# A quarter-by-quarter second product put ahead of the next batch, with the loads in another order

## The chip, the cores and the metric

The kernel runs on one core of one Trainium2 chip. The metric is the device time of one execution in microseconds, and the median of several runs is given. A profile is one more execution, with every instruction and every DMA packet recorded.

The engines are TensorE (PE in the profile; PEld is its weight loads), VectorE (DVE), ScalarE (ACT), GpSimd (POOL) and SyncE (SP). They run side by side and wait for each other by semaphores. In this kernel SP issues the loads of q, k and v and the DMA transpositions, and POOL issues the loads of the weights and most of the output stores.

## The reference

Eight batches go through a linear attention and then a mixer. Cut to what is computed:

```python
# attention: batch, heads, seq, head_dim = 8, 8, 576, 64
r = max(x, 0);  phi(x) = concat(r * cos_w, r * sin_w)       # for q and for k, cos_w and sin_w by position
kv  = einsum('bhsf,bhsd->bhfd', phi(k), v)
num = einsum('bhsf,bhfd->bhsd', phi(q), kv)
den = einsum('bhsf,bhf->bhs', phi(q), sum(phi(k), axis=2)) + 1e-6
x   = num / den                                             # heads side by side: (8, 576, 512)
# mixer: U (576, 32), V (32, 576), w_ch1 (512, 2048), w_ch2 (2048, 512)
u   = x + (x^T @ U @ V)^T
out = u + max(u @ w_ch1, 0) @ w_ch2
```

Inputs and output are float32; the kernel multiplies in bfloat16 and sums in float32.

## The kernel before

**Tiles.** The 576 rows of a batch are four chunks of 128 (c = 0 to 3, row 4p + c on partition p) and a tail of 64 (c = 4). Tails of two batches share the partitions of one tile, so batches go in pairs (`pr`, batches `e` = 2 pr and `o` = 2 pr + 1).

**Attention of a batch** is made of units:
- `q_prep` and `k_prep` (two instructions each, one with the cosine and one with the sine, on the engines that the call names), `v_prep` or `v_block` (casts of v into `v_ext`, which has a column of ones, so that kv also holds the sum over phi(k)).
- `qtr_unit`: eight transpositions of a chunk of q on PE and one evacuation. `kv_unit`: 20 small products for four heads.
- x, in one of two ways. `x_unit` makes all eight heads of a chunk with 65 columns each, so the denominators come with the numerators; `den_unit` and `xh_unit` make the denominators of all chunks first, with 20 one-column products, and then x for four heads at a time.
- `A_unit` (x^T U, four column groups of PE side by side), `u_unit` (A V and the sum with x), and u transposed for the next product, either by PE (`uTd_open`, `uTd_mm`, `uTd_evac`: x transposed, A V added in the same accumulator) or by a DMA (`utr_dma`). `uTt_direct` does the pair's tail on PE.

**The mixer.** `g1_main(b, j)` is one of 16 units of the first product of a batch: four matmuls of 128x512, then the evacuation with the relu by ACT into `hid`. It needs the j-th 128 columns of `w1_bf`, which is loaded in quarters (`w1_load(n)`, columns for four units each). `g1_tail` does four units for both tails. `g2_part(pr, cc, p)` is a quarter of the second product for one chunk: four matmuls with four of the 16 row blocks of `w2_bf`, which is loaded in quarters too (`w2_load(n)`). After the fourth part DVE adds u and a DMA stores the result. Both weights are cast to bfloat16 by the DMA, so that a quarter is 0.52 MB in the core and 1.05 MB outside.

**Order.** The schedule is written out by hand: instructions of an engine run in the order in which the code calls them. First comes batch 0's attention (`chain_head`, `chain_mid`, `chain_end`), with `keep_warm` products on zeros between. Then a list of slots runs: for each pair 16 units of `g1_main` for the even batch, 16 for the odd, four of `g1_tail`, and 36 of `g2_part` (nine chunks by four parts), 72 slots in all. After each slot the calls stand that are attached to it: those of `beside` (batch 1) and those that `attention_plan` derives from `PLAN` (batches 2 to 7: the slot of the first kv unit, then the offsets of the casts, the transpositions and the next batch's loads). In the first pair slots 8 to 12 are empty, since batch 1's chain, called at slot 7, holds these five units inside itself (`fill1`).

**Memory for sums.** Eight PSUM banks: tag "o" has two buffers, "g" three, "T" one, and "X" one of two banks. A unit names the tag that it takes, and waits until the buffer's last reader is done.

**Loads.** q, k and v of a batch have one buffer each (`qst`, `kst`, `vst`, with the tails in `qt`, `kt`, `vt`), so the next batch's load waits until the casts have read the last. SP issues them in the order of the code. POOL issues the weights: the first quarter of `w1` once k of batch 0 has landed (a copy into `mark`, line 685, waits for it), the second after batch 0's chain head, which on POOL means after the casts of U and V (`cast_uv`); the third and fourth after a copy that waits for the transposed tail of batch 1's q (line 722); the quarters of `w2` after one that waits for batch 1's v (line 724). A one-element DMA into `mark2` (line 647) holds batch 2's loads back on SP until batch 1's second denominators are made.

Of the kernel before, what the change touches and what calls it, by code (L numbers as in the profile page):

```python
# [10 lines left out]
FP32 = mybir.dt.float32  # L11
# [6 lines left out]
def kernel(  # L18
# [11 lines left out]
    nc = tc.nc  # L30
# [31 lines left out]
    def alloc_k(b):  # L62
        kst[b] = pool.tile([P, H, 4, D], FP32, tag="kst", bufs=1, name="kst")
        kt[b] = pool.tile([P, H, D], FP32, tag="kt", bufs=1, name="kt")
# [9 lines left out]
    def load_main(dst, src, b, h0=0, h1=H, eng=None):  # L74
        (eng or nc.sync).dma_start(
            out=dst[:, h0:h1, :, :].rearrange("p h c d -> p h (c d)"),
            in_=src[b, h0:h1, 0:512, :].rearrange("h (p c) d -> p h (c d)", c=4),
        )

    def load_tail(dst, src, b, eng=None):  # L80
        (eng or nc.sync).dma_start(  # L81
            out=dst[tail(b), :, :],
            in_=src[b, :, 512:S, :].rearrange("h s d -> s h d"),
        )
# [4 lines left out]
    def w1_load(n):  # L89
        cs = slice(n * 512, n * 512 + 512)  # L90
        nc.gpsimd.dma_start(
            out=w1_bf[:, :, cs], in_=moe_w_ch1.rearrange("(d p) n -> p d n", p=P)[:, :, cs]
        )
# [36 lines left out]
    load_tail(vt[0], v, 0)  # L130
    load_main(vst[0], v, 0, 0, 4)
    load_main(vst[0], v, 0, 4, 8)
    for i in range(4):
        nc.sync.dma_start(out=stV[i * R : i * R + R, :], in_=moe_V)
    nc.sync.dma_start(
        out=stU[:, 0:4, :], in_=moe_U[0:512, :].rearrange("(p c) r -> p c r", c=4)
    )
    for lo in (0, TS):
        nc.sync.dma_start(out=stU[lo : lo + TS, 4, :], in_=moe_U[512:S, :])
    zero = const.tile([P, 512], BF16)  # L140
    V_.memset(zero, 0.0)
    halfpi = const.tile([P, 1], FP32)
# [33 lines left out]

    V_.memset(U_bf, 0.0)
    mark = const.tile([TS, 1], FP32)
    mark2 = const.tile([1, 1], FP32)

    def cast_uv():
        cast(G_, U_bf[:, 0:4, :], stU[:, 0:4, :])
        for i in range(2):
            cast(G_, U_bf[tail(i), 4 + i, :], stU[tail(i), 4, :])
        cast(G_, V_bf, stV[:, 0:512].rearrange("r (p c) -> r c p", c=4))
        cast(G_, V_tl, stV[:, 512:S])
# [242 lines left out]
    def uTd_close(b, d, eng):  # L429
        uTd_mm(b, d)  # L430
        uTd_evac(b, d, eng)
# [75 lines left out]
    def g2_part(pr, cc, part):  # L507

        last = pr == NPAIR - 1 and cc == 8
        if part == 0 or last and part == 3:  # L510
            o_ps[pr, cc] = ps.tile([P, DM], FP32, tag="o", bufs=2, name="o_ps")
        o = o_ps[pr, cc]
        if cc == 4:
            b, lhs, c, u = None, hid_tl[pr], 0, u_tl[pr]
        else:
            b, c = (2 * pr, cc) if cc < 4 else (2 * pr + 1, cc - 5)
            lhs, u = hid[b], u_bf[b][:, c, :]

        if last:
            cols = slice(0, 384) if part < 3 else slice(384, DM)  # L520
            js = (range(0, 5), range(5, 10), range(10, NJ), range(NJ))[part]
        else:
            cols, js = slice(0, DM), range(part * 4, part * 4 + 4)
        for j in js:
            nc.tensor.matmul(  # L525
                out=o[:, cols],
                lhsT=lhs[:, j, c * P : c * P + P],
                rhs=w2_bf[:, j, cols],
                start=(j == 0),
                stop=(j == NJ - 1),  # L530
            )
        if js[-1] < NJ - 1:
            return
        o_sb = pool.tile([P, DM], FP32, tag="o_sb", bufs=4, name="o_sb")
        nc.vector.tensor_tensor(  # L535
            out=o_sb[:, cols], in0=u[:, cols], in1=o[:, cols], op=ALU.add
        )
        eng = nc.gpsimd if pr < NPAIR - 1 else nc.scalar if part == 3 and last else nc.sync
        if cc == 4:
            for i in range(2):  # L540
                eng.dma_start(
                    out=out[2 * pr + i, 512:S, :], in_=o_sb[i * TS : i * TS + TS, :]
                )
        else:
            eng.dma_start(  # L545
                out=out[b, 0:512, cols].rearrange("(p c) n -> p c n", c=4)[:, c, :],
                in_=o_sb[:, cols],
            )
# [20 lines left out]
    ORD = (4, 0, 1, 2, 3)  # L569

    def spare(at):

        return ("o", 2) if at % 72 < 36 else ("g", 3)


# [1 line left out]

    QORD = (4, 0, 1, 2, 3)
    PLAN = {
        2: (42, -22, V_, V_, -14, (-8, -8, -8)),  # L580
        3: (58, -17, A_, A_, -10, (6, 6, 6)),
        4: (100, -20, V_, V_, -12, (-6, -6, -6)),
        5: (130, -20, A_, A_, -13, (-7, -7, -7)),
        6: (172, -20, V_, V_, -12, (-6, -6, -6)),
# [39 lines left out]
    def chain_head(b, fill, xt, engs):  # L624
        v_prep(b, 0, 4, (4,), (engs[0],))
        v_block(b, 0, 4, 0, 3, V_)
        v_block(b, 0, 4, 3, 4, engs[0])
        kv_unit(b, 0, "T", 1)
        fill(0)
        rec0 = den_unit(b, 0, 4, "X", 1)  # L630
        v_prep(b, 4, 8, (4,), (A_,))
        v_block(b, 4, 8, 0, 4, A_)
        fill(1)
        for n, c in enumerate(ORD):
            xh_unit(b, c, 0, 4, rec0, *xt[n])
            if n == 1:
                fill(2)
            if n == 3:
                kv_unit(b, 1, "T", 1, A_)

    def chain_mid(b, fill, xt, dt):
        fill(3)
        m = 3 if b == 0 else 2
        rec1 = den_unit(b, 4, 8, *dt)
        if b == 1:

            nc.sync.dma_start(out=mark2, in_=rec1[0:1, 0, 0:1])
        for n, c in enumerate(ORD[:m]):
            xh_unit(b, c, 4, 8, rec1, *xt[n])
        u01 = ps.tile([P, 2, 512], FP32, tag="X", bufs=1, name="u01")  # L650
        uTd_open(b, 0, None, None, u01[:, 0, :].rearrange("p (c t) -> p c t", c=4))
        uTd_open(b, 1, None, None, u01[:, 1, :].rearrange("p (c t) -> p c t", c=4))
        a0 = A_unit(b, "T", 1, A_, 0, 256)
        fill(4)
        uTd_mm(b, 0)
        uTd_mm(b, 1)
        uTd_evac(b, 0, A_)
        uTd_evac(b, 1, A_)
        for n, c in enumerate(ORD[m:]):
            xh_unit(b, c, 4, 8, rec1, *xt[m + n])  # L660
        fill(5)
        return a0
# [21 lines left out]

    G_.tensor_copy(out=mark, in_=kt[0][0:TS, 0, 0:1])
    w1_load(0)
    cast_uv()
    chain_head(0, warm0, (O2, O2, G3, G3, O2), (A_,))
    w1_load(1)
    alloc_q(1)  # L690
    load_main(qst[1], q, 1)
    load_tail(qt[1], q, 1)
    alloc_k(1)
    load_main(kst[1], k, 1)
    load_tail(kt[1], k, 1)
    alloc_v(1)
    load_tail(vt[1], v, 1)
    load_main(vst[1], v, 1, 0, 4)
    load_main(vst[1], v, 1, 4, 8)
    a0 = chain_mid(0, warm0, (O2, G3, O2, G3, O2), G3)  # L700
    chain_end(0, a0)
    g1_main(0, 0, True)
# [10 lines left out]
    def at(j, *thunks):  # L713
        beside.setdefault(j, []).extend(thunks)

    for n, c in enumerate(ORD):
        if n > 1:
            at(n - 2, lambda c=c, n=n: q_prep(1, c, (V_, A_ if n % 2 == 0 else V_)))
        tg = ("T", 1) if n % 2 else O2
        at(1 + n, lambda c=c, tg=tg: qtr_unit(1, c, eng=V_, tag=tg[0], bufs=tg[1]))  # L720
        at((4, 5, 5, 6, 6)[n], lambda c=c, n=n: k_prep(1, c, (V_, A_)))
    at(2, lambda: G_.tensor_copy(out=mark, in_=q_tlT[0:TS, 0, TS : TS + 1]))
    at(2, lambda: [w1_load(2), w1_load(3)])
    at(6, lambda: G_.tensor_copy(out=mark, in_=vst[1][0:TS, 0, 0, 0:1]))
    at(6, lambda: [w2_load(n) for n in range(4)])
    st1 = {}

    def fill1(n):
        if n in (0, 4):
            u_unit(0, 0 if n == 0 else 1, "o", 2)  # L730
        if n > 0:
            g1_main(0, 7 + n)

    xt1 = (O2, O2, O2, O2, O2)
    at(7, lambda: chain_head(1, fill1, xt1, (V_,)))
    at(7, lambda: st1.update(a=chain_mid(1, fill1, xt1, ("T", 1))))
    at(7, lambda: chain_end(1, st1["a"]))
    at(13, lambda: uTd_close(1, 2, V_), lambda: uTd_close(1, 3, A_))

    slots, todo = [], {}  # L740
    for pr in range(NPAIR):
        e, o = 2 * pr, 2 * pr + 1
        slots += [
            (lambda: None) if pr == 0 and 8 <= j < 13 else lambda j=j, e=e: g1_main(e, j)
            for j in range(NJ)
        ]
        slots += [lambda j=j, o=o: g1_main(o, j) for j in range(NJ)]
        slots += [lambda j=j, pr=pr: g1_tail(pr, j) for j in range(4)]
        slots += [
            lambda cc=cc, p=p, pr=pr: g2_part(pr, cc, p) for cc in range(9) for p in range(4)  # L750
        ]
    for j, ts_ in beside.items():
        todo[j] = list(ts_)
# [1 line left out]
    def put(at, thunk):  # L755
        todo.setdefault(at, []).append(thunk)

    put(17, lambda: uTt_direct(0, "o", 2, V_))
    for n, (b, c) in enumerate([(0, 2), (0, 3)] + [(1, c) for c in ORD]):
        put(18 + n, lambda b=b, c=c: u_unit(b, c, *spare(18)))  # L760
    for n, t in enumerate(loads(2, nc.sync)):
        put((9, 12, 13)[n], t)
    for b in range(2, B):
        for at, t in attention_plan(b):
            put(at, t)
# [34 lines left out]
```

## Time and profile before

| | |
|---|---|
| median of 3 runs | 319.39 us (317.74 to 320.44) |
| the profiled execution: time, span | 320.26 us, 318.5 us |
| PE busy | 306.9 us, 96% of the span |
| DVE, ACT, POOL busy | 148.2, 145.8, 45.7 us |
| largest groups on PE | first product 119.7 us, second product 119.2 us (line 525) |
| moved by DMA | 53.30 MB, 167 GB/s in the mean |

The span reaches from the first to the last instruction of the program. The profiled execution is a little above the median of the timed ones, so a sum made from its rows is set against its own time. PE's busy share is that of the whole span; what the stages lose is seen only in windows. Times in a timeline are from the span's start. The first unit of `g1_main` starts at 23.6 us, the odd batch's first at about 53 us, the pair's tails at 69.2, the second product at 73.0, and the second pair at 110.4.

### The profile page before, as it was taken

The page shows a single profiled execution, that of the slowest core. Times are in us where ns is not written, and L with a number is a line of the kernel's source. Part 1 is how long each engine was busy: PE and PEld are TensorE (multiplying, and loading weights), DVE is VectorE, ACT ScalarE, POOL GpSimd, SP SyncE. Part 2 cuts the span into 40 slices and gives each one's busy share as a digit, 9 for nine tenths or more (in the row PEclk, how much of TensorE's full clock was granted, in tenths as well). Part 3 has the DMA queues.
Part 4 walks back from the last instruction along what each step waited for, and adds up shares of the span by engine and source line. Part 5 has one row for each costly group of instructions (what it writes and reads, how often), then busy time and mean ns, then how long its engine had stood idle before and what let it go on. Part 6 is the DMA issues. An engine that isn't in the chain of part 4 may idle for free.

```text
span 318.5 us, 5777 instructions
## 1 busy us (share of the span) xinstructions
PE 306.9 (96%) x2372; PEld 160.0 (50%) x2372; DVE 148.2 (47%) x325; ACT 145.8 (46%) x241; POOL 45.7 (14%) x85
## 2 busy tenths in 40 slices
PE   8697799999999999999999999999999999999996
PEld 3464464465545444476445444475445444464443
DVE  6667753880567659125615667025525640001211
ACT  4735836567800056658900056659700256650000
POOL 1132400400420113001421220002321100000000
PEclk9999989999999999999999999999999999999999
DMA  7999999579674899952399539911491130001122
GB/s 233 264 303 282 191 188 320 154 174 323 201 178 118 277 306 181 286 176 19 114 240 348 207 97 201 344 69 51 127 205 66 68 82 0 2 0 68 66 91 74
DMA packets 88603, 53.30 MB, mean 167 GB/s; under 512 B 56642, under 2 KB 85698, under 8 KB 88578
## 3 DMA queue, kind: packets, MB, share of 16 engines
q1 hardware_dynamic: 82002, 41.61, 48.6%
q0 software_dynamic: 6432, 11.27, 14.8%
q8 instruction: 18, 0.29, 0.4%
q10 hardware_dynamic: 144, 0.07, 0.1%
q14 instruction: 7, 0.06, 0.1%
HBM read 37.08 MB, written 9.44 MB: 146 GB/s over the span
## 4 chain that ended last, share of the span: by engine, by line
PE 87%; DMA 7%; DVE 2%; SPq 2%; POOL 0%; issue 0%; DVEq 0%; POOLq 0%
PE o_ps L525 39%; PE g_ps L473 34%; PE gt_ps L493 4%; DMA w_bf<-in_moe_w_ch_dram 3%; DMA vst<-in_v_dram 3%; PE kv_ps L246 3%; PE x_ps L340 2%; PE va_ps L385 2%; DMA st_uv<-in_moe_U_dram 2%; SPq L81 1%; PE a_ps L365 1%; DVE k_p L214 1%; DVE v_ext L105 0%; PE va_ps L388 0%; DVE q_pT L105 0%; PE xh_ps L322 0%
## 5 line engine op out<-in xcount | busy, mean ns | idle before, releaser
L482 ACT ACTIVATE hid<-g_ps 128x512 bf16<-128x512 f32 x128 | 76.3, 597 | 117.8 <-PE g_ps L473 117.7
L473 PE MATMUL g_ps<-uT,w_bf 128*128 128x512 bf16 x512 | 119.7, 383 | 1.9 <-DMA w_bf<-in_moe_w_ch_dram 1.9
L525 PE MATMUL o_ps<-w_bf,hid 128*128 128x512 bf16 (+2 forms) x528 | 119.2, 372 | 0.0
L473 PEld LDWEIGHTS <-w_bf 128*128 128x128 bf16 x512 | 48.9, 98 | 59.4 <-issue 2.8
L525 PEld LDWEIGHTS <-hid 128*128 128x128 bf16 x528 | 48.5, 98 | 51.4 <-issue 0.8
L535 DVE TENSOR_TENSOR o_sb<-u_bf,o_ps 128x512 f32<-128x512 bf16 (+2 forms) x33 | 22.1, 669 | 60.1 <-PE o_ps L525 60.0
L545 POOL DMA_DIRECT2D out_dram<-o_sb x24 | 13.2, 549 | 141.2 <-DVE o_sb L535 65.0
L392 DVE TENSOR_TENSOR u_bf<-x_bf,va_ps 128x512 bf16<-128x512 bf16 x32 | 21.9, 685 | 10.1 <-PE va_ps L385 10.0
L105 DVE CAST kv<-kv_ps 128x260 bf16<-128x260 f32 x14 | 6.0, 429 | 35.8 <-PE kv_ps L246 35.8
L350 DVE TENSOR_TENSOR x_bf<-x_ps,rec 128x512 bf16<-128x512 f32 x24 | 16.6, 691 | 0.8
L105 POOL CAST v_ext<-vst 128x512 bf16<-128x512 f32 x24 | 15.1, 663 | 6.0 <-DMA vst<-in_v_dram 4.2
L493 PE MATMUL gt_ps<-uT_tl,w_bf 128*128 128x128 bf16 x256 | 15.6, 219 | 0.0
L297 DVE TENSOR_SCALAR rec<-x_ps 128x8 f32<-128x8 f32 (+1 forms) x30 | 5.0, 166 | 22.7 <-PE x_ps L340 22.3
L246 PE MATMUL kv_ps<-v_ext,k_p 128*128 128x65 bf16 x256 | 11.9, 193 | 3.4 <-DVE v_ext L105 3.4
L493 PEld LDWEIGHTS <-w_bf 128*128 128x128 bf16 x256 | 14.7, 98 | 0.9
L246 PEld LDWEIGHTS <-k_p 128*128 128x128 bf16 x256 | 11.2, 97 | 7.1 <-ACT v_ext L103 2.1
L525 PE MATMUL o_ps<-w_bf,hid_tl 128*128 128x512 bf16 x64 | 14.8, 379 | 0.0
L175 PE MATMUL w_ps<-zero 128*128 128x512 bf16 x40 | 11.9, 432 | 1.8 <-DVE halfpi L143 1.2
L212 ACT ACTIVATE k_p<-kst,sinw 128x512 bf16<-128x512 f32 x19 | 13.1, 710 | 1.1 <-DMA kst<-in_k_dram 1.1
L212 ACT ACTIVATE q_p<-qst,sinw 128x512 bf16<-128x512 f32 x17 | 11.9, 711 | 3.7 <-DMA qst<-in_q_dram 3.7
L385 PE MATMUL va_ps<-A_sb,V_bf 128*128 128x512 bf16 x32 | 12.1, 379 | 0.1
L500 ACT ACTIVATE hid_tl<-gt_ps 128x512 bf16<-128x512 f32 x16 | 9.6, 598 | 5.8 <-PE gt_ps L493 5.8
(103 smaller groups left out, 243.0 us busy)
## 6 DMA issues: line engine op xcount, KB each, us to landing
qst<-in_q_dram SPq DMA_DIRECT2D x8, 1024.0 KB, 6.8
kst<-in_k_dram SPq DMA_DIRECT2D x8, 1024.0 KB, 9.1
vst<-in_v_dram SPq DMA_DIRECT2D x6, 1024.0 KB, 9.0
out_dram<-o_sb POOLq DMA_DIRECT2D x24, 256.0 KB, 3.6
w_bf<-in_moe_w_ch_dram POOLq DMA_DIRECT2D x8, 512.0 KB, 10.3
vst<-in_v_dram SPq DMA_DIRECT2D x4, 512.0 KB, 9.9
out_dram<-o_sb SPq DMA_DIRECT2D x7, 256.0 KB, 2.3
qt<-in_q_dram SPq DMA_DIRECT2D x8, 128.0 KB, 4.2
```

The costliest lines, as they stand in the source:

```text
L105: eng.tensor_copy(out=o, in_=i)
L212: nc.scalar.activation(out=o, in_=i, func=AF.Relu, bias=0.0, scale=w)
L246: nc.tensor.matmul(out=acc[:, i, :], lhsT=k_p[b][:, c, h, :] if c < 4 else k_tl[:, h, :], rhs=vx[:, c, h, :], start=(c == 0), stop=(c == 4),)
L350: nc.vector.tensor_tensor(out=x_of(b, c, rows).rearrange("p (g i d) -> p g i d", g=2, d=D), in0=view[:, :, :, 0:D], in1=rec[rows].unsqueez ...
L385: nc.tensor.matmul(out=va, lhsT=V_bf[:, c, :], rhs=A_of(b), start=True, stop=True)
L392: nc.vector.tensor_tensor(out=u_bf[b][:, c, :] if c < 4 else u_tl[b // 2], in0=x_of(b, c), in1=va, op=ALU.add,)
L473: nc.tensor.matmul(out=g_ps.rearrange("p (c t) -> p c t", c=4), lhsT=w1_bf[:, d, j * P : j * P + P], rhs=uT[b][:, :, d, :], start=(d == 0) ...
L482: nc.scalar.activation(out=hid[b][:, j, :], in_=g_ps, func=AF.Relu, bias=0.0, scale=1.0)
L493: nc.tensor.matmul(out=g_ps[:, jj, :], lhsT=w1_bf[:, d, j * P : j * P + P], rhs=uT_tl[pr][:, d, :], start=(d == 0), stop=(d == 3),)
L525: nc.tensor.matmul(out=o[:, cols], lhsT=lhs[:, j, c * P : c * P + P], rhs=w2_bf[:, j, cols], start=(j == 0), stop=(j == NJ - 1),)
L535: nc.vector.tensor_tensor(out=o_sb[:, cols], in0=u[:, cols], in1=o[:, cols], op=ALU.add)
L545: eng.dma_start(out=out[b, 0:512, cols].rearrange("(p c) n -> p c n", c=4)[:, c, :], in_=o_sb[:, cols],)
```

## The change

Six things are changed.

1. Batch 0's second product for its four full chunks (16 of the 36 parts) comes right after batch 0's first product, in slots 16 to 31, ahead of batch 1's first product (now slots 32 to 47). It runs by quarters of `w2`: part 0 of all four chunks, then part 1, and so on. So four accumulators are open at once: two under "o" and two under "g". The other 20 parts follow after `g1_tail`, in slots 52 to 71.
2. Batch 1's attention is no longer a chain with units of g inside. k is cast in slots 9 to 13 on DVE and ACT, and v in slot 15 on DVE alone; the two kv units stand at slots 16 and 17, five x units at 18 to 26, A at 27, the transpositions at 28 and 29.
3. The loads: two quarters of `w1` are issued before the casts of U and V and two right after them, with no wait for q. k's tail goes ahead of k. v waits for q's tail (a one-element DMA into `mark3`) and is one load instead of two halves. The quarters of `w2` wait for k's tail instead of v.
4. Batch 2's loads stand at slot 15, behind a one-element DMA that reads the second quarter of `w2` (`gate`).
5. V, and the last rows of U, are loaded with one DMA each instead of four and two.
6. `PLAN` moves batches 2 and 3 by four slots, with other offsets; the pair's tail of u is transposed by a DMA (slot 33) instead of `uTt_direct`; some tags differ (`spare`).

```diff
-    for i in range(4):
-        nc.sync.dma_start(out=stV[i * R : i * R + R, :], in_=moe_V)
+    nc.sync.dma_start(out=stV, in_=moe_V.unsqueeze(0).to_broadcast([4, R, S]))
...
-    for lo in (0, TS):
-        nc.sync.dma_start(out=stU[lo : lo + TS, 4, :], in_=moe_U[512:S, :])
+    nc.sync.dma_start(
+        out=stU[:, 4, :], in_=moe_U[512:S, :].unsqueeze(0).to_broadcast([2, TS, R])
+    )
...
-            o_ps[pr, cc] = ps.tile([P, DM], FP32, tag="o", bufs=2, name="o_ps")
+            tag, bufs = ("g", 3) if pr == 0 and 2 <= cc < 4 else ("o", 2)
+            o_ps[pr, cc] = ps.tile([P, DM], FP32, tag=tag, bufs=bufs, name="o_ps")
...
     def spare(at):
+        if at < 72:
+            return ("o", 2) if 32 <= at < 52 else ("g", 3)
...
-        2: (42, -22, V_, V_, -14, (-8, -8, -8)),
-        3: (58, -17, A_, A_, -10, (6, 6, 6)),
+        2: (46, -15, V_, V_, -10, (-5, -5, -5)),
+        3: (62, -14, V_, A_, -10, (6, 6, 6)),
...
     w1_load(0)
+    w1_load(1)
     cast_uv()
+    w1_load(2)
+    w1_load(3)
     chain_head(0, warm0, (O2, O2, G3, G3, O2), (A_,))
-    w1_load(1)
     alloc_q(1)
     load_main(qst[1], q, 1)
     load_tail(qt[1], q, 1)
     alloc_k(1)
+    load_tail(kt[1], k, 1)
     load_main(kst[1], k, 1)
-    load_tail(kt[1], k, 1)
+    nc.sync.dma_start(out=mark3, in_=qt[1][TS : TS + 1, 0, 0:1])
     alloc_v(1)
     load_tail(vt[1], v, 1)
-    load_main(vst[1], v, 1, 0, 4)
-    load_main(vst[1], v, 1, 4, 8)
+    load_main(vst[1], v, 1)
+    G_.tensor_copy(out=mark, in_=kt[1][TS : 2 * TS, 0, 0:1])
+    for n in range(4):
+        w2_load(n)
...
-            at(n - 2, lambda c=c, n=n: q_prep(1, c, (V_, A_ if n % 2 == 0 else V_)))
+            at(n - 2, lambda c=c: q_prep(1, c, (V_, V_)))
...
-        at((4, 5, 5, 6, 6)[n], lambda c=c, n=n: k_prep(1, c, (V_, A_)))
-    at(2, lambda: G_.tensor_copy(out=mark, in_=q_tlT[0:TS, 0, TS : TS + 1]))
-    at(2, lambda: [w1_load(2), w1_load(3)])
-    at(6, lambda: G_.tensor_copy(out=mark, in_=vst[1][0:TS, 0, 0, 0:1]))
-    at(6, lambda: [w2_load(n) for n in range(4)])
...
-    at(7, lambda: chain_head(1, fill1, xt1, (V_,)))
-    at(7, lambda: st1.update(a=chain_mid(1, fill1, xt1, ("T", 1))))
-    at(7, lambda: chain_end(1, st1["a"]))
-    at(13, lambda: uTd_close(1, 2, V_), lambda: uTd_close(1, 3, A_))
+        at(9 + n, lambda c=c: k_prep(1, c, (V_, A_)))
+        at(15, lambda c=c, n=n: v_prep(1, 0, H, (c,), ((V_, V_, V_, V_, V_)[n],)))
+        at(18 + 2 * n, lambda c=c: x_unit(1, c, "X", 1))
+    for c in range(4):
+        at(5 + c, lambda c=c: u_unit(0, c, *O2))
+    for hg in range(2):
+        at(16 + hg, lambda hg=hg: kv_unit(1, hg, "T", 1))
...
+    at(27, lambda: A_unit(1, "T", 1, A_))
+    at(28, open1)
+    at(29, close1)
+    for n, c in enumerate(ORD):
+        at((32, 44, 45, 46, 47)[n], lambda c=c: u_unit(1, c, *O2))
+    at(33, lambda: utr_dma(1, 4, 5))
...
+        early = [(cc, p) for p in range(4) for cc in range(4)] if pr == 0 else []
+        slots += [lambda cc=cc, p=p: g2_part(0, cc, p) for cc, p in early]
...
-    put(17, lambda: uTt_direct(0, "o", 2, V_))
-    for n, (b, c) in enumerate([(0, 2), (0, 3)] + [(1, c) for c in ORD]):
-        put(18 + n, lambda b=b, c=c: u_unit(b, c, *spare(18)))
+    put(15, lambda: gate(w2_bf[0:1, 4, 0:1]))
     for n, t in enumerate(loads(2, nc.sync)):
-        put((9, 12, 13)[n], t)
+        put(15, t)
```

`open1` transposes batch 1's x for three of the four 128-column groups of u, `close1` the fourth, and then adds A V to all four and evacuates them by DVE and ACT in turn.

## The prediction

> **What bounds the kernel now.** First the page's busy times and its 40 slices:
>
> ```profile
> PE 306.9 (96%) x2372; PEld 160.0 (50%) x2372; DVE 148.2 (47%) x325; ACT 145.8 (46%) x241; POOL 45.7 (14%) x85
> ...
> PE   8697799999999999999999999999999999999996
> ...
> PEclk9999989999999999999999999999999999999999
> DMA  7999999579674899952399539911491130001122
> ```
>
> TensorE (PE) is the bound, and all that it loses lies in the first seven slices. So I read that stretch by windows (stretch and its length, busy us and count of PE, PEld, DVE, ACT, POOL, then granted clock, DMA share, GB/s):
>
> ```profile
> 24.00:56.00 32.00, 27.69 (x286) 15.88 (x285) 18.56 (x41) 19.85 (x34) 5.66 (x8) 0.95 1.14 246
> 56.00:315.00 259.00, 259.00 (x1850) 132.35 (x1847) 113.34 (x239) 113.35 (x186) 35.09 (x60) 1.00 0.55 150
> 36.00:40.00 4.00, 2.75 (x44) 1.76 (x45) 2.60 (x7) 2.95 (x5) 1.05 (x2) 0.87 1.13 170
> 40.00:44.00 4.00, 4.00 (x49) 2.43 (x48) 1.92 (x5) 1.58 (x3) 0.00 (x0) 0.71 1.17 186
> 50.00:58.00 8.00, 8.00 (x53) 4.00 (x51) 2.67 (x5) 4.72 (x9) 0.00 (x0) 1.00 1.10 356
> ```
>
> From 56 us to 315 PE is never idle: nothing is to be won there except by fewer instructions. From 24 to 56 it is idle for 4.3 us, and at 36 to 44 the clock drops. The DMA engines are full all that time (share above 1). Third, the timeline, for the waits:
>
> ```profile
> 25.14 0.49 DVE L214 TENSOR_SCALAR q_tl<-qt,cosw 64x512 bf16<-64x512 f32 x1
> 26.16 0.61 PE L263 MATMUL t_ps<-ident,q_tl 128*128 128x128 bf16 x8
> 30.86 1.04 PE L473 MATMUL g_ps<-uT,w_bf 128*128 128x512 bf16 x4 [1.91 <-DMA w_bf<-in_moe_w_ch_dram]
> 36.90 0.49 PE L246 MATMUL kv_ps<-v_ext,k_p 128*128 128x65 bf16 x4 [1.52 <-DVE v_ext L105]
> ```
>
> The two large waits are both for loads: the second quarter of w_ch1, and batch 1's v. So the prediction turns on when each load lands in the new order. The last view is that of a tile's transfers, here the second half of batch 1's v (issue, then time to landing):
>
> ```profile
> L75 SPq DMA_DIRECT2D vst<-in_v_dram x1: 2933/2933/2933, 24.5 to 24.5; - x1
> ...
> DMA to landing us min/median/max: 12.8/12.8/12.8
> ```
>
> Its 0.52 MB needs 1.5 us at 356 GB/s, yet it lands at 37.3, because quarters of w_ch1 issued on POOL's queue at 27.7 and 28.4 run beside it. SP's loads lose heavily to the weights on the other queue.
>
> **What the change gains.** (1) The idle time of 24 to 56, 32.00 - 27.69 = 4.3 us. (2) The clock: 4 us at 0.87 and 4 at 0.71 cost 0.5 + 1.2 = 1.7 us. (3) Work: batch 1 by x units needs no denominator products (two groups of 20, 38.39 to 39.03 and 44.36 to 45.00 in the timeline, 1.3 us), and the pair's tail is transposed by a DMA instead of 12 products (54.96 to 55.39, 0.4 us): 1.7 us. All three lie on PE's path, since nothing but PE sets the end. Together 7.7 us.
>
> **What it costs.** (a) *Batch 1's q.* Before, w_ch1's second quarter was issued at 21.2, and the third and fourth only after q had been used (27.7). Now POOL issues two quarters at 12.8 and 13.9, and two more after the casts of U and V (about 19 to 21), so all four stand against q, which SP can issue once k of batch 0 has landed, about 12.7. The bounds: as before, 6.6 us from issue (the row of q's load at 16.6), 19.3 and no wait; or behind all of w_ch1. A quarter takes 2.55 us alone (w_ch2's first and third land at 42.9 and 48.0), so from 15.5, when the first begins to flow, four take until 25.7, and q and its tail (1.18 MB at 356 GB/s) another 3.3: 29.0, with some 2 us for the engine that finishes last 31.0. The nearest row is v's half: issue 12.7 + 12.8 = 25.5, and q with its tail is 0.66 MB longer, 1.9 us alone and about double beside the weights: 29.0. I take that. In the code qt is needed first: cosine on DVE, sine on ACT, then the transposition, 1.0 us after DVE's start (25.14 to 26.16 above). PE reaches it at 26.2, so it waits 29.0 + 1.0 - 26.2 = 3.8 us (0 to 5.8). Behind the waiting casts stand the rest of q on DVE and, on ACT, the evacuations of the first two g units; PE could not have used either, as its transposition is next in its own order.
>
> (b) *The clock* after that wait: the same 1.7 us as in the row of 36 to 44, where 1.5 us of idle and thin work came first (0 to 1.7, and twice if a second long wait follows).
>
> (c) *Batch 1's v.* PE's work from the transposition to the first kv unit: half a g unit 0.43, thirteen at 0.86 (11.2), five transpositions at 0.45 (26.16 to 26.61), four u units at 0.22 (two g units with one between are 1.08 apart at 60.1 to 61.2), one quarter product of 0.86: 15.7, so it arrives at 26.2 + 3.8 + 1.7 + 15.7 = 47.4. v is issued when qt has landed (29.0), behind k, and beside w_ch2, which POOL issues when kt has landed. Half of v took 12.8 us so; the whole with its tail is again 0.66 MB more, alone 1.9, doubled 3.4: 29.0 + 12.8 + 3.4 = 45.2. Five casts on DVE (128x256 of v took 0.48, 128x768 0.56; 0.42 each is my middle) add 2.1: 47.3, so no wait is left. The bounds: 39 without contention, and 50.5, when before the same bytes had all landed (the last quarter, issued at 36.0, took 14.5). At 50.5 PE starts kv at 52.6: with 41.9 for an unhindered arrival, waits of 10.7 us in all, q's wait included.
>
> (d) *Small waits.* The first A product follows the last x unit by one part of 0.86, and x needs 0.17 + 0.28 + 0.69 on DVE: 0.4 us with a semaphore's way. In units 9 to 13 ACT does an evacuation of 0.60 and a k cast of 0.71 to each 0.86 of PE, 2.2 us behind after five, of which three g buffers cover two units, 1.7: 0.5 us. Together 0.9 (0 to 2).
>
> **What costs nothing, and why.** V and U go in three DMAs instead of seven: they land earlier, but the first product's chain waits for x and A as well, so I count no gain. The four accumulators hold two g buffers from unit 18 to 31; in that time only one uT tile uses the third. The first output stores and the sums with u fall in units 28 to 31, 0.69 on DVE each to 0.86 of PE. The part products need w_ch2's quarters at units 16, 20, 24, 28; if these come 2.55 to 4 us apart after about 39, they are ahead of PE, which needs over 3.5 for each. Batch 2's loads wait on SP for w_ch2's second quarter (about 43 instead of 46 before for the first issue); behind that wait stand only these loads, first used after unit 31, at some 64. The DMA transposition of the tail (2.3 us to landing) has 14 units of cover. Batches 2 and 3 move four units later; batch 2's last uT transposition, 2.8 us to landing, has six units (over 5 us).
>
> **The sum.** 318.5 - 7.7 + 3.8 + 1.7 + 0.0 + 0.9 = 317.2 us of span. The profiled execution took 320.26 with 318.5 of span, so 1.8 lies around it: 319.0. It stood 0.9 above the median of 319.39; against that the forecast is 318.1.
>
> **Two rules of the Trainium skill.** The trace shows v's half 12.8 us under way beside the weights. "DMA: Bandwidth & Descriptors", section "Queues, rings and completion order", says that an engine drains a whole packet, typically 9 to 17 descriptors, from one queue before it turns to the next. It speaks against this change: by it q would come after nearly all of w_ch1, at the upper bound of 31.0, and the time would be some 2 us longer. The clock fell to 0.71 after an idle of 1.5 us with thin work behind. "TensorE: Matmul & The Clock Gate", section "HAM oscillation", asks for an idle of over some 3.4 us before the clock drops; by it the 1.7 us of (b) might stay away in a wait of 3.8 that straddles two of its windows.
>
> **Rivals.** *The loads keep out of each other's way* (chance 0.36). For it: SP issues q four microseconds earlier than before, and k's tail is put ahead of k so that w_ch2 follows early. Against it: v's half above. Price: without (a), (b), (c) the span is 318.5 - 7.7 + 0.9 = 311.7, 312.6 against the median; with 2.5 us of waits 315.1.
>
> *v of batch 1 comes last of all* (0.27), the case that ends slower. One mechanism: w_ch2's quarters are on POOL's queue when v is issued, and v's half has already been seen to wait for weights; PE stands at the kv unit after part product 16 with nothing else to do. It decides from a landing of about 48: then kv starts at 50.1, 8.2 us behind the unhindered 41.9, and 8.2 + 1.7 + 0.9 - 7.7 is 3.1 us over before. At 50.5 it is 10.7 + 1.7 + 0.9 - 7.7 = 5.6 over: 325.0.
>
> *The change does not reorder what matters*: w_ch2's first quarter is later than v, so the early product stalls itself. It is issued before v flows, so I give it no chance of its own; it would cost as the last case.
>
> **How the numbers follow.** The forecast, waits that give back most of the gain, 0.37, with its own range 315.5 to 321.5. A measurement of this kernel can tell about 1% from no change, that is 3.2 us: faster below 316.2, slower above 322.6. Faster 0.36, same 0.37, slower 0.27, from the three cases. The range reaches from the first rival's end, 312.6, to near the second's: 312.5 to 324.5.
>
> **What would show it.** A wait of PE for q_tl at about 26 (right: 2 to 6 us; wrong: none), a dip of the clock after it, no wait of PE for w_ch1, a wait at the first kv unit of batch 1 under 2 us, and after unit 32 a PE without gaps. A first kv unit of batch 1 before 43 us makes the first rival true; after 50, the second. Gaps past 70 us would make wrong what I cost at nothing.

## The result, and the profile after

The changed kernel takes 322.03 us in the median of 17 runs (320.31 to 323.38), the kernel before 318.88 us on the same chips (17 runs, 317.25 to 320.45). The ratio is 1.0096, interval 1.0072 to 1.012: about 1% slower, where the forecast of 318.1 stood 1.3 us below the 319.39 of before, so even the direction was wrong. The profiled execution took 323.38 us with a span of 321.6.

The page of the changed kernel, the busy times and the 40 slices:

```profile
PE 304.7 (95%) x2285; PEld 158.7 (49%) x2312; DVE 153.4 (48%) x340; ACT 135.9 (42%) x225; POOL 50.6 (16%) x84
...
PE   8766999999999997999999999999999999999995
...
PEclk9995999999999999999999999999999999999999
DMA  7999999958997899993299949981492140001131
```

PE's records are 87 fewer than before, but its weight loads are only 60 fewer: 27 products of this trace have no record, 22 of them of the second product (line 527). So the 2.2 us by which PE is busy less can't be set against the 1.7 that were forecast. The low digits stand in slices 1 to 3 (8 to 32 us), earlier than I looked for them, one granted clock of 0.5 follows in slice 3, and there is a 7 in slice 15 (120 to 128 us). The windows (stretch, length, busy us and count of PE, PEld, DVE, ACT, POOL, granted clock, DMA share, GB/s):

```profile
24.00:56.00 32.00, 28.52 (x219) 15.30 (x223) 18.11 (x39) 14.95 (x26) 6.26 (x11) 0.89 1.08 217
56.00:315.00 259.00, 255.75 (x1840) 131.11 (x1860) 119.29 (x258) 109.81 (x181) 41.06 (x60) 1.00 0.67 155
24.00:28.00 4.00, 0.72 (x6) 0.51 (x8) 0.00 (x0) 0.39 (x1) 2.01 (x5) 0.68 0.76 171
28.00:32.00 4.00, 4.00 (x31) 2.06 (x30) 1.18 (x3) 1.08 (x2) 1.09 (x2) 0.50 1.17 220
25.48:32.30 6.82, 5.01 (x36) 2.62 (x38) 1.18 (x3) 1.47 (x3) 3.29 (x7) 0.50 1.05 211
```

From 24 to 28 us PE works 0.72 of 4 us, and from 25.48 to 32.30 all passes at half the clock. From 56 to 315 its records leave 3.25 us idle, where they had left none: a wait of 1.9, one of 0.2, and 22 gaps of 0.05 us each, as many as there are products of line 527 without a record. So these gaps, 1.2 us in all, are not time that PE lost. What it waited for, from the view of waits (us in total, times, longest):

```profile
PE a_ps L372 <- POOL U_bf L105: 3.5, 1, 3.5
PE g_ps L474 <- DMA uT<-u_bf: 1.9, 1, 1.9
...
PE u L439 <- POOL V_bf L105: 1.2, 1, 1.2
PE a_ps L366 <- POOL U_bf L105: 1.0, 1, 1.0
```

Not q, not w_ch1, not batch 1's v: PE waits 5.7 us for the casts of U and V in batch 0's own chain (21.3 to 27.5 us), which I had costed at nothing, and 1.9 us at 128.7 for batch 3's transposed u. The timeline of POOL says why the casts are late (start, length, what, in brackets the idle time before and what ended it):

```profile
22.03 0.29 POOL L105 CAST U_bf<-st_uv 128x128 bf16<-128x128 f32 x1 [7.42 <-DMA st_uv<-in_moe_U_dram]
25.86 0.47 POOL L105 CAST U_bf<-st_uv 64x32 bf16<-64x32 f32 x2 [3.54 <-DMA st_uv<-in_moe_U_dram]
26.40 1.08 POOL L105 CAST V_bf<-st_uv 128x512 bf16<-128x512 f32 x1
```

And in the kernel before:

```profile
19.68 0.21 POOL L105 CAST U_bf<-st_uv 64x32 bf16<-64x32 f32 x1 [1.31 <-DMA st_uv<-in_moe_U_dram]
```

That of SP's queue, the last DMA of U and batch 1's q behind it:

```profile
11.12 0.59 SPq L137 DMA_DIRECT2D st_uv<-in_moe_U_dram  x1
11.84 4.56 SPq L75 DMA_DIRECT2D qst<-in_q_dram  x1
16.50 6.03 SPq L81 DMA_DIRECT2D qt<-in_q_dram  x1
```

And in the kernel before:

```profile
13.38 1.84 SPq L139 DMA_DIRECT2D st_uv<-in_moe_U_dram  x2
16.60 0.39 SPq L75 DMA_DIRECT2D qst<-in_q_dram  x1
17.10 0.62 SPq L81 DMA_DIRECT2D qt<-in_q_dram  x1
```

POOL stands twice for the DMAs of U, which were issued before 12 us, and casts at 22.0 and 25.9. In the kernel before they were issued by 15.2, and the last cast of U ran at 19.7. The issues of batch 1's q on SP take 4.6 and 6.0 us instead of 0.4 and 0.6.

### The profile page after: what moved, and what is told of

It reads as the page before. It is cut to its first block, busy times and chain, and to the rows that moved or that the text cites. A ratio compares the mean times of both kernels' runs of the same rounds, so it can differ in the third digit from the quotient of the medians.

```text
span 321.6 us, 5612 instructions
## 1 busy us (share of the span) xinstructions
PE 304.7 (95%) x2285; PEld 158.7 (49%) x2312; DVE 153.4 (48%) x340; ACT 135.9 (42%) x225; POOL 50.6 (16%) x84
## 2 busy tenths in 40 slices
DMA packets 89043, 53.43 MB, mean 166 GB/s; under 512 B 57082, under 2 KB 86138, under 8 KB 89018
## 4 chain that ended last, share of the span: by engine, by line
PE 79%; DMA 7%; DVE 5%; SPq 4%; issue 2%; ACT 1%; POOL 1%; DVEq 0%; POOLq 0%
PE o_ps L527 38%; PE g_ps L474 27%; DMA st_uv<-in_moe_U_dram 4%; PE gt_ps L494 3%; PE x_ps L341 3%; DVE q_p L215 3%; PE kv_ps L247 2%; DMA qst<-in_q_dram 2%; PE va_ps L386 2%; SPq L81 2%; SPq L75 1%; DMA uT<-u_bf 1%; PE a_ps L366 1%; PE t_ps L264 1%; ACT hid L483 1%
## 5 line engine op out<-in xcount | busy, mean ns | idle before, releaser
L474 PE MATMUL g_ps<-uT,w_bf 128*128 128x512 bf16 x512 | 118.2, 380 | 2.0 <-DMA uT<-u_bf 1.9
L527 PE MATMUL o_ps<-w_bf,hid 128*128 128x512 bf16 (+2 forms) x509 | 117.9, 372 | 0.9
L393 DVE TENSOR_TENSOR u_bf<-x_bf,va_ps 128x512 bf16<-128x512 bf16 x32 | 21.9, 685 | 11.9 <-PE va_ps L386 10.7
L351 DVE TENSOR_TENSOR x_bf<-x_ps,rec 128x512 bf16<-128x512 f32 x28 | 19.3, 691 | 1.0
L298 DVE TENSOR_SCALAR rec<-x_ps 128x8 f32<-128x8 f32 (+1 forms) x35 | 5.8, 165 | 24.0 <-PE x_ps L341 23.5
L105 POOL CAST v_ext<-vt 64x512 bf16<-64x512 f32 x6 | 10.1, 1682 | 29.9 <-DMA vt<-in_v_dram 18.5
L341 PEld LDWEIGHTS <-q_pT 128*128 128x128 bf16 x224 | 10.7, 98 | 6.6 <-DVE x_bf L351 0.7
L215 DVE TENSOR_SCALAR q_p<-qst,cosw 128x512 bf16<-128x512 f32 x24 | 12.3, 525 | 1.9 <-DMA qst<-in_q_dram 1.8
```

The source lines that it names most:

```text
L105: eng.tensor_copy(out=o, in_=i)
L215: eng.tensor_scalar(out=o, in0=i, scalar1=0.0, scalar2=w, op0=ALU.max, op1=ALU.mult)
L341: nc.tensor.matmul(out=acc[:, g, i * E : i * E + E], lhsT=qT_of(b, c, h), rhs=kv_sb[b][:, h, :], start=True, stop=True,)
L351: nc.vector.tensor_tensor(out=x_of(b, c, rows).rearrange("p (g i d) -> p g i d", g=2, d=D), in0=view[:, :, :, 0:D], in1=rec[rows].unsqueez ...
L393: nc.vector.tensor_tensor(out=u_bf[b][:, c, :] if c < 4 else u_tl[b // 2], in0=x_of(b, c), in1=va, op=ALU.add,)
L474: nc.tensor.matmul(out=g_ps.rearrange("p (c t) -> p c t", c=4), lhsT=w1_bf[:, d, j * P : j * P + P], rhs=uT[b][:, :, d, :], start=(d == 0) ...
```

## The experiments

In the expectations the theories have letters or short names; A is that the two broadcast DMAs are the cost. Each ratio is against runs of the kernel before that were made together with it on the same chip. The table puts the runs side by side: the start of batch 1's first kv unit, PE's waits of 0.2 us and more between 20 us and that unit, the granted clock from 24 to 56, the largest wait later on, for a u transposed by DMA where nothing else is said. In e1, e2, e7, e8 and e11 the clock is at half for some time before 24 us too, which the column of the clock does not show.

| kernel | ratio (interval) | span | first kv | waits before it | clock | later wait |
|---|---|---|---|---|---|---|
| after | 1.0096 (1.0072, 1.012) | 321.6 | 50.25 | U, V 5.7 | 0.89 | 1.9 |
| e1 | 1.0227 (1.018, 1.0274) | 323.6 | 51.0 | A_sb 0.5, q 1.1, v 4.9 | 0.89 | 0.5 |
| e2 | 1.005 (1.002, 1.0079) | 317.2 | 46.9 | U, V 3.5, w_ch1 0.3 | 0.93 | 0.7 (for ACT) |
| e3 | 1.0058 (1.0019, 1.0097) | 319.9 | 49.2 | V 0.5, q 0.7, w_ch1 3.8 | 0.95 | 1.2 |
| e5 | 1.0148 (1.0083, 1.0213) | 316.8 | 47.2 | V 0.7, q 2.6, w_ch2 1.2 | 0.95 | 0.5 |
| e6 | 1.0026 (0.9999, 1.0053) | 316.8 | 47.2 | V 2.0, w_ch1 2.3 | 0.95 | 0.5 |
| e7 | 1.006 (1.0033, 1.0087) | 318.1 | 47.5 | U, V 3.6, q 0.2 | 0.93 | 1.0 |
| e8 | 1.0224 (1.0183, 1.0264) | 321.6 | 49.8 | U, V 6.4, q 0.2 | 0.88 | 2.6 |
| e9 | 0.9954 (0.9925, 0.9982) | 313.8 | 42.7 | V 1.9 | 1.00 | 0.4 |
| e10 | 1.0044 (1.0015, 1.0074) | 316.3 | 43.2 | V 0.5, q 1.3, other 0.2 | 1.00 | 2.4 |
| e11 | 1.0187 (1.0148, 1.0226) | 322.5 | 48.4 | U, V 5.7 | 0.91 | 2.1 |

The profiles are of runs within 1.4 us of their kernel's median, but for e5's, which is of its fastest (318.55, median 321.33): that row understates.

**e1: the broadcasts split again.**

```diff
-    nc.sync.dma_start(out=stV, in_=moe_V.unsqueeze(0).to_broadcast([4, R, S]))
+    for i in range(4):
+        nc.sync.dma_start(out=stV[i * R : i * R + R, :], in_=moe_V)
...
-    nc.sync.dma_start(
-        out=stU[:, 4, :], in_=moe_U[512:S, :].unsqueeze(0).to_broadcast([2, TS, R])
-    )
+    for lo in (0, TS):
+        nc.sync.dma_start(out=stU[lo : lo + TS, 4, :], in_=moe_U[512:S, :])
```

> The changed kernel with V loaded in four DMAs and the last rows of U in two, as before; the two early quarters of w_ch1 stay ahead of the casts. Theory A (in the changed kernel V's one DMA and the one of U's last rows run on a few of the 16 DMA engines, where each packet takes turns with the weights, so the casts of U and V end at 27.6 instead of 21.2 us and PE waits 5.7 us for them): the casts end by 22.5, PE's waits for U_bf and V_bf fall below 1 us, the first unit of g starts before 26 instead of 31.0; q may then be the next wait, so the time falls by 3 to 7 us, to 315 to 319. Theory B (the second quarter of w_ch1, issued at 13.8 ahead of the casts, is what delays U and V, however they are cut): the waits for U_bf and V_bf stay above 4 us and the time stays within 1 us of the changed kernel's 322.

325.56 us, not better. From its waits:

```profile
PE kv_ps L247 <- DVE v_ext L105: 7.8, 2, 4.9
...
PE t_ps L264 <- ACT q_tl L213: 1.1, 1, 1.1
...
PE u L439 <- ACT A_sb L103: 0.5, 1, 0.5
```

The waits for U and V are gone (their casts end at 22.7), so the broadcasts did cause them. But PE now reaches the kv unit of batch 1 at 46.1 and stands 4.9 us for v, which landed at 50.49. So v was late in the changed kernel too (48.48), hidden by the earlier wait. Splitting alone moves the wait. Why the time is above the changed kernel's is not wholly shown: the profile also has 2.9 us of wait for batch 0's v before 17 us (1.7 in the changed kernel's), which lies ahead of the casts that the edit touches, and half the clock from 18.2 to 21.7.

**e2: the second quarter of w_ch1 behind the casts.**

```diff
     w1_load(0)
-    w1_load(1)
     cast_uv()
+    w1_load(1)
     w1_load(2)
```

> The changed kernel with the second quarter of w_ch1 issued after the casts of U and V, as before; V and the last rows of U stay in one DMA each. Theory A: V's packets take turns with the first quarter alone and the last rows of U follow without contention, so the casts end 2 to 3 us earlier than 27.6, not at 21.2; PE's waits for U_bf and V_bf keep 2 to 4 of their 5.7 us; 319 to 321. Theory B: the casts end by 22, the waits are gone; 314 to 318.

320.09 us. The wait for U and V falls from 5.7 to 3.5, v lands at 44.61, and kv starts 3.3 us earlier. With a quarter of w_ch1 less beside them the broadcasts end sooner, but still not in time.

**e3: both edits.**

> The changed kernel with both undone: seven DMAs for V and U, and the second quarter of w_ch1 after the casts. Both theories: the casts of U and V end at 21 to 22 as before the change, no wait of PE for them, the first unit of g at 23.6 to 24.5. It shows what the rest of the change is worth: 314 to 318 if q lands early enough (by 27), 318 to 321 if PE then waits for q or for the second quarter of w_ch1.

321.01 us. One line of its waits:

```profile
PE g_ps L474 <- DMA w_bf<-in_moe_w_ch_dram: 3.8, 1, 3.8
```

The freed time is lost at w_ch1's second quarter, which landed at 34.3 behind q.

**e4: the kernel before, with the two broadcast DMAs** (the diff of e1 reversed).

> The kernel before, with nothing changed but V and the last rows of U in one DMA each. Theory A: V's packets on their few engines take turns with the first quarter of w_ch1, the casts end at 23.5 to 25 instead of 21.2, w_ch1's second quarter is issued later by as much, and the time rises by 2 to 4 us, to 321 to 323. Theory B: the four and two DMAs were no part of it; within 0.7 us of before.

319.22 us, ratio 1.001 (0.9977 to 1.0043). PE waits 2.6 us for U and V there, but its wait of 1.9 for w_ch1 (30.9 in the profile of before) is gone. What is late first hides what would be late next; so the edit is free in the old schedule, and that says nothing of the new one.

**e5: e1, with w_ch2 issued only when v has landed.**

```diff
-    G_.tensor_copy(out=mark, in_=kt[1][TS : 2 * TS, 0, 0:1])
+    G_.tensor_copy(out=mark, in_=vst[1][0:TS, 0, 0, 0:1])
```

> The changed kernel with V and U in seven DMAs (e1_split_uv), and the quarters of w_ch2 issued only when batch 1's v has landed. In e1_split_uv PE waited 4.9 us for v at the first kv unit, and v, issued at 30.8 beside w_ch2, landed at 50.5. Theory C (v and w_ch2 share the DMA engines turn by turn, and whichever comes second stops PE, since batch 1's kv units and the early product want both at unit 16): v lands at 40 to 43 and its wait is gone, but w_ch2's first quarter lands at 47 to 50 instead of 42.7, so PE now waits 2 to 5 us for w_bf at the first part product; 321 to 326, no gain against e1_split_uv's 325.6 beyond 4 us. Theory D (v alone is too late, w_ch2 has slack): the wait for v is gone and nothing takes its place; 318 to 320.

321.33 us, a ratio 0.8% below e1's, though with four runs of each the intervals overlap. v lands at 40.22 instead of 50.49 and its wait is gone: batch 1's v does pay for the w_ch2 quarters beside it, as the prediction's second rival had it. PE waits 2.6 for q and 1.2 for w_ch2 instead.

**e6: the new order of products with the loads of before** (seven DMAs for U and V, w_ch1's second quarter behind the casts, its other two after batch 1's transposed q tail, v in halves, w_ch2 after v).

```diff
+    at(2, lambda: G_.tensor_copy(out=mark, in_=q_tlT[0:TS, 0, TS : TS + 1]))
+    at(2, lambda: [w1_load(2), w1_load(3)])
+    at(6, lambda: G_.tensor_copy(out=mark, in_=vst[1][0:TS, 0, 0, 0:1]))
+    at(6, lambda: [w2_load(n) for n in range(4)])
```

> The changed kernel's order of work with all of the loads of batch 1 and of the weights issued in the order and with the waits of the kernel before (V and U in seven DMAs; w_ch1's second quarter after the casts, third and fourth after q is used; v in two halves; w_ch2 after v has landed). Theory E (it is the order of the loads that costs, not the order of the products): q lands by 24, v by 38, w_ch2's first quarter at 43; the first kv unit starts at 43 to 45 instead of 50.3, and the time is 314 to 317, below both kernels. Theory F (the new order of products costs by itself, for instance by four open accumulators or by batch 2 and 3 being moved): the kv unit starts early but the time stays above 318.

317.84 us, no different from before. So the loads, and not the order of products, make the changed kernel slower; yet the order alone gains nothing, as the old loads cost it 4.3 us of waits and a clock of 0.95.

**e7: the changed kernel with a quarter of w_ch1.**

```diff
     def w1_load(n):
+        if n > 0:
+            return
...
-                lhsT=w1_bf[:, d, j * P : j * P + P],
+                lhsT=w1_bf[:, d, j % 4 * P : j % 4 * P + P],
```

> The changed kernel, but only the first quarter of w_ch1 is loaded, and all sixteen units of the first product read its four column blocks again (three quarters, 3.1 MB, are left out; the products are as many and as large). If the loads alone take the gain back, TensorE then meets U and V, q and v with little or no wait: the sum of the prediction without its load terms has the first kv unit of batch 1 at 41.9 us, and with 1 to 2 us left for U and V it starts at 42 to 44; the span is 269.5 us and the later wait of 1.9 more, 313.5 to 315.5, a ratio of 0.98 to 0.99 against the kernel before. If the new order of products is itself slow (DVE and ACT, the accumulators), the first kv unit stays at 48 us or later and the time at 319 or more.

319.44 us: a miss for both, the first kv unit stood at 47.5 (42 to 44 in the one, 48 or later in the other). Three quarters of the weight are left out, and PE still waits 3.6 us for U and V (the first rows of U are cast at 21.9) and then runs at 0.93. So the sum of bytes is not what decides, and the two broadcasts with one quarter of w_ch1 beside them are enough for most of the wait.

**e8: batch 3 two slots earlier.**

```diff
-        3: (62, -14, V_, A_, -10, (6, 6, 6)),
+        3: (60, -14, V_, A_, -10, (6, 6, 6)),
```

> The changed kernel with one number other: batch 3's attention stands two slots earlier (60 instead of 62). If the 1.9 us that TensorE waits for batch 3's transposed u at 128.7 us lies on the path, it goes, and the time is some 1.9 us below the changed kernel's, a ratio of 1.002 to 1.006 against the kernel before. If the wait only moves (to another unit of batch 3, or is paid at the end), the ratio stays at 1.008 to 1.011. The stretch before 56 us should not change.

324.55 us, ratio 1.0224, and the wait at 128.66 us is 2.6 instead of 1.9. A miss. The offsets in `PLAN` are counted from batch 3's slot, so batch 4's loads move with it and stay ahead of the transpositions on SP. In the timeline of SP the transpositions of batch 3's u are issued from 116.8 to 126.1 right behind the six loads of batch 4, which land until 125.9.

**e9: loads and casts arranged for the new order.** On e1:

```diff
     w1_load(3)
+    w2_load(0)
     chain_head(0, warm0, (O2, O2, G3, G3, O2), (A_,))
...
-    load_main(vst[1], v, 1)
-    G_.tensor_copy(out=mark, in_=kt[1][TS : 2 * TS, 0, 0:1])
-    for n in range(4):
+    load_main(vst[1], v, 1, 0, 4)
+    load_main(vst[1], v, 1, 4, 8)
+    G_.tensor_copy(out=mark, in_=vst[1][0:TS, 0, 0, 0:1])
+    for n in range(1, 4):
         w2_load(n)
...
-        at(1 + n, lambda c=c, tg=tg: qtr_unit(1, c, eng=V_, tag=tg[0], bufs=tg[1]))
+        at(5 + n, lambda c=c, tg=tg: qtr_unit(1, c, eng=V_, tag=tg[0], bufs=tg[1]))
...
-        at(15, lambda c=c, n=n: v_prep(1, 0, H, (c,), ((V_, V_, V_, V_, V_)[n],)))
+        at(15, lambda c=c: v_prep(1, 0, 4, (c,), (V_,)))
+        at(16, lambda c=c: v_prep(1, 4, 8, (c,), (V_,)))
```

The casts of q go four slots later as well, and the u units of batch 0 from slots 5 to 8 to slots 1 to 4.

> The changed order of products, with loads and casts arranged for it: U and V in seven DMAs, the first two quarters of w_ch1 ahead of their casts, the other two and the first of w_ch2 behind them, q used four slots later (the u units of batch 0 take its place), v in two halves of heads cast in two parts, the last three quarters of w_ch2 after the first half. If the waits at q_tl, w_ch1 and v are a matter of which load is asked for first, they go: a first kv unit of batch 1 at 43 to 45 us and a span of 313.5 to 315.5, a ratio of 0.984 to 0.993. If the sum of bytes sets the time (8.4 MB from 16.5 us on, before the first kv unit can end), the waits only change their names and the first kv unit stays at 47 us, a ratio of 0.998 to 1.005.

315.64 us, ratio 0.9954 (0.9925 to 0.9982): faster than both kernels. Kv unit and span are about as the first theory had them, the ratio is a smaller gain than its 0.984 to 0.993. Its waits and the window:

```profile
PE u L439 <- POOL V_bf L105: 1.9, 1, 1.9
...
PE kv_ps L247 <- DVE v_ext L105: 0.5, 2, 0.3
```

```profile
24.00:56.00 32.00, 31.33 (x248) 16.82 (x246) 20.77 (x52) 13.46 (x23) 3.03 (x5) 1.00 1.06 207
```

The kv unit starts at 42.7, and the clock never falls. The DMA share and the bytes are those of the changed kernel (53.43 MB): only which load is asked for when, and when it is needed, has changed.

**e10: e9 with batch 3 two slots earlier** (the diff of e8).

> The last kernel, with batch 3 two slots earlier as well (60). If the wait for batch 3's transposed u is still there in that kernel (0.5 to 1.9 us), this one is that much faster; else the two are the same within 0.3%.

318.85 us, 3.2 above e9: neither expectation. One line of its waits; in the timeline it stands at 107.87 us, at the first unit of the second pair, where batch 2's u is needed:

```profile
PE g_ps L474 <- DMA uT<-u_bf: 2.4, 1, 2.4
```

Batch 2's last transposition is issued 1.3 us later than in e9 (100.8) and lands 7.0 us after its issue instead of 3.7. That batch 3's work, moved forward, is in its way is likely, but what delays the transposition is not shown. Another 1.3 us stands at q, ahead of what the edit touches. Slot 62 is better than 60 here; what place would be best is open.

**e11: e9 with the two broadcast DMAs put back.**

> The kernel e9_loads_for_order with one thing put back: V and the last rows of U in one broadcast DMA each, as in the changed kernel. If these two DMAs, with two quarters of w_ch1 beside them, are what makes TensorE wait for the casts of U and V, that wait is back at 4 to 6 us (1.9 in e9), the clock falls after it (1.00 from 24 to 56 us in e9, about 0.9 here), and the first kv unit of batch 1 moves from 42.7 to 47 to 50 us: a ratio of 1.005 to 1.015, some 1 to 2% above e9. If the order of the loads is all that counts, the time stays at e9's 0.995.

324.22 us, 8.6 above e9's median; the spans differ by 8.7 (another chip, with the kernel before at 317.38 there and 317.22 beside e9). Its waits, window and casts:

```profile
PE a_ps L372 <- POOL U_bf L105: 4.6, 1, 4.6
PE g_ps L474 <- DMA uT<-u_bf: 2.1, 1, 2.1
...
PE u L439 <- POOL V_bf L105: 1.2, 1, 1.2
PE kv_ps L247 <- DVE v_ext L105: 1.1, 2, 0.9
```

```profile
24.00:56.00 32.00, 28.89 (x223) 15.45 (x227) 19.29 (x45) 14.93 (x26) 6.49 (x11) 0.91 1.03 195
```

```profile
25.28 0.47 POOL L105 CAST U_bf<-st_uv 64x32 bf16<-64x32 f32 x2 [4.77 <-DMA st_uv<-in_moe_U_dram]
```

```profile
20.84 0.21 POOL L105 CAST U_bf<-st_uv 64x32 bf16<-64x32 f32 x1 [2.74 <-DMA st_uv<-in_moe_U_dram]
```

The second of these lines is e9's: the cast that runs at 20.84 there runs at 25.28 here. PE idles 5.7 us for U and V instead of 1.9, the clock falls to 0.91, and kv starts at 48.4 instead of 42.7. Two DMAs in place of six are the only difference of the programs, so the loss is theirs, with what follows from them: the 2.1 us that PE waits for batch 3's u, and a second stretch at half clock behind that wait (128.89 to 132.30), which costs another 1.7.

**e12: the changed kernel once more.**

> The changed kernel once more, on the chip and beside the runs of e11. It gave 1.0096 (1.0072 to 1.012) first, and the one number changed in e8 made it 1.0224. If batch 3's place is what cost that, the ratio here is 1.007 to 1.012 again. If the ratio of the changed kernel differs from chip to chip by this much, it is 1.015 to 1.025 here, and e8 says nothing of batch 3.

322.42 us, ratio 1.0134 (1.0095 to 1.0173), with 6.9 us of waits for U and V, a clock of 0.87 and a first kv unit at 50.1. It overlaps the first result, and its interval ends just below where e8's begins (1.0183). So batch 3's two slots seem to cost something in e8 as in e10, but weakly: the runs are of two chips, and e8's profile and this one have the same span of 321.6.

## Why the prediction was wrong

*The gains (7.7 us)* are there in kind. From the first kv unit's start take off the waits, and half of the time that PE works at half the clock: 50.25 - 5.7 - 2.5 = 42.1 is left in the changed kernel, 42.7 - 1.9 = 40.8 in e9, 47.2 - 4.3 - 1.7 = 41.2 in e6. This is the unhindered arrival, forecast as 41.9. But the profile that I summed from was of a run of 320.26 us, while runs of before spread from 315.38 to 320.08 beside e9. Their granted clocks tell them apart: 14 of those 29 have a mean clock of 0.999 or 1.0 and take 316.4 us in the mean, 14 have 0.993 to 0.995 and take 318.0 (the last, 0.989 and 320.08). The run of the profile has 0.995. So the clock's 1.7 us can be won in about half of the runs of before only, and e9, whose span is 4.7 below that of the profile of before, is 1.6 us below before in the medians (315.64 to 317.22).

*"V and U go in three DMAs instead of seven: they land earlier ... I count no gain"* is the step that failed. They were issued earlier and landed later, and the chain behind them had no slack: a term put at nothing cost 5.7 us of waiting, and the dip of the clock came with it. I looked at the issues on SP (3.3 us for four copies of V) and not at the transfer. e1, e11 and e9 show that the broadcast form is the cause, e2 that the second quarter of w_ch1 beside it adds to it. It was not the only step: e1 shows that without it v would have come next, 4.9 us.

*(a) q, 3.8 us*: its tail qt landed at 31.23 and not at 29.0, but PE came later still and did not wait. In e1, without the first wait, it landed at 29.10 and cost 1.1. The prediction drew its upper bound of 31.0 from the Trainium skill's rule on whole packets too, but a change of queue after each packet is no reason for q to come after nearly all of w_ch1; and here another cause stands in the trace, SP's issue of qt being held up until 22.5, so this is no test of the rule.

*(b) the clock, 1.7 us*: mis-sized. It is at half for 6.8 us, of which PE works 5.0, so half of that is lost, 2.5 us. In all runs the stretches at half clock last 3.4 us or two or three times that, but for those that the program's end cuts short. "TensorE: Matmul & The Clock Gate", section "HAM oscillation", of the Trainium skill wants over 3.4 us of idle before a drop. These runs differ, and the measurement decides: in the changed kernel the clock fell 2.8 us into the wait of 3.45, and in e5, e6 and e11 it fell within 0.9 us after single waits of 2.6, 2.3 and 2.1. After e8's wait of 2.6 at 128.66 it did not fall. So the length of a wait alone does not settle it. The stretch after the wait in e11, and two after that in e8:

```profile
128.89:132.30 3.41, 3.41 (x10) 1.21 (x9) 0.36 (x1) 1.19 (x2) 3.07 (x5) 0.50 1.28 170
...
127.20:130.60 3.40, 1.94 (x9) 0.90 (x10) 1.42 (x4) 0.61 (x2) 3.40 (x4) 1.00 0.97 192
130.60:134.00 3.40, 3.40 (x17) 1.56 (x16) 0.00 (x0) 2.38 (x4) 0.72 (x2) 1.00 1.18 146
```

*(c) v*: forecast to land at 45.2 (with 1.9 doubled to 3.8, and not 3.4, 45.6) and to cost nothing. It landed at 48.48, and kv started at 50.25 without a wait, which is past the mark of 50 that I had set for the second rival. That this rival's time came out nearly right (3.1 us over before at a landing of 48) is luck: the 8.3 us by which kv is behind 41.9 are U, V and the clock (5.7 and 2.5), none of them v, and where the rival added another 1.7 for the clock, 1.9 stood at 128.7. Its mechanism came second: v is the next wait, shown by e1 and taken away in e5.

*(d) small waits, 0.9 us*: none. From 27.5 to 56 us no gap of PE in the changed kernel is over 0.06 us.

*"Batches 2 and 3 move four units later"* at no cost: 1.9 us at 128.67, where batch 3's transpositions stand on SP behind batch 4's loads. No run moves these loads alone, so that they are its cause is argued and not shown.

The sum with the measured terms: 318.5 - 7.7 + 5.7 + 2.5 + 0.0 + 1.9 + 0.2 = 321.1 of span, against 321.6 (0.2 is the small wait between 56 and 315); 0.5 us stays unaccounted for.

## What to carry to other kernels

When several loads are late, the profile shows only the first one that PE meets; price the next in line, and test a load's edit in the schedule in which it will run (e4 free, e11 8.6 us). Fewer DMAs are not an earlier landing: look at how the packets flow before counting an earlier issue as a gain. A reordering of products pays only when each load's issue, and each consumer's slot, are moved with it (e6 nothing, e9 0.5%).

## What the runs showed of the hardware

The packet records tell the two forms of V's load apart. V is 128 packets of 2304 bytes in both. In e9 (four DMAs) 44 and 49 of them start in the first two half microseconds, and all are through by 16.4 us; in the changed kernel (one broadcast) mostly 10 to 16 start in each, and the last goes at 20.4. From 15.5 us on 57 to 80 packets of w_ch1 start beside them, but the first 12 and 16 of V had 2 and 21 beside them, so the low rate is not made by w_ch1. Added up over the records, 3.6 packets of V are in flight in the mean, and 10.8 in e9. The load with fewer packets in flight, not fewer bytes, is the slow one. The 128 packets of 128 bytes of U's last rows go mostly 11 to 13 to the half microsecond, and the last at 25.4 us.

A rate of a quarter fits what the Trainium skill says in "DMA: Bandwidth & Descriptors", section "Why a DMA increments its semaphore by 16 and not by 1": a DMA is spread over the largest number of engines up to 16 that divides the slowest dimension of both patterns. By it the broadcast of V, with 4 as its outer dimension, goes over 4 engines and that of U over 2. For V the trace agrees, not only by the 12 packets against 46. A packet's record does not name its engine, but the load behind V on SP's queue, of U's first 512 rows, shows it: 96 of its 128 packets start by 16.9 us, and the other 32, a quarter, only from 19.9 on, when V's last packets go. In all seven kernels with the broadcasts these 128 packets split into 96 and, after a gap of 2.0 to 4.7 us, 32; in none with four DMAs do they. So U's first rows, no broadcast themselves, are late because a quarter of them waits behind V. For U's last rows no count here shows the 2.
